# Two layers of feature-map attention and a gated unit: row sums for seven slabs by one TensorE operation, with a realignment through DRAM

## The chip, the cores and the metric

One core of one Trainium2 chip runs the whole program. The metric is the device time of one execution in microseconds (us). Three executions of the kernel before took 391.33, 390.58 and 389.74 us (median 390.58). The profiled execution took 390.76 us; its span, from the first to the last instruction, is 389.0 us.

## What is computed

The input x has 2048 rows of 512 columns in bf16. Attention (A) and a gated unit (B) alternate, twice each, with the same weights in both layers:

```python
x = A_x
x = x + A(layernorm(x)); x = x + B(layernorm(x))
x = x + A(layernorm(x)); x = x + B(layernorm(x))
# A, 32 heads of width 16:
q, k, v = split(x @ wqkv)
pq, pk = q @ w_phi[h], k @ w_phi[h]
phi(p) = concat(softmax(p), softmax(-p))            # 32 features per head
kv, z = phi(pk)^T @ v, sum over rows of phi(pk)
A(x) = ((phi(pq) @ kv) / (phi(pq) @ z + 1e-6)) @ wo
# B, inner width 1376:
B(x) = (relu(x @ W_gate) * (x @ W_up)) @ W_down
```

The sums kv and z run over all 2048 rows, so the query side of a layer can't be ended before the key side of all its rows is done.

## The kernel before

**Tiles and slabs.** The 2048 rows are 16 tiles of 128, grouped in five slabs of 2, 4, 4, 4 and 2 tiles (L15); slab 0 has 256 rows, slab 1 has 512, slab 4 has 256. I write (0,2) for slab 2 of the first layer. x stays in SBUF (`x_sb`).

**The start.** The loads are issued at L708 to L730. w_phi is folded into the key and query weights by `fold` (L777): each of four column blocks of the weight has to be transposed, either by TensorE with an eviction (L783, L784, from a natural copy in `hT`) or by a transposing DMA issued on SyncE's queue (L702); the list XW says which blocks the DMA takes (L181: blocks 0 and 1 of the key weight, all four of the query weight). The block-diagonal form `BD` of w_phi is made at L762, and the products of L789 are evicted to `Wkp` and `Wqp` at L791.

**The key side** (`into_a`, L1238). Layer norm (L813: statistics on VectorE at L798, scale and shift on ScalarE at L840 or VectorE at L843) writes `ytile`. It is transposed into `yA` or `yG` by DMA (L848) or by TensorE (L677 with L855, L872 with L878). `keys` (L883) makes key and value products of a tile, the two exponentials on ScalarE (L900), sums of 16 on VectorE (L906), reciprocals on VectorE (L909) or as Ln and Exp on ScalarE (L912, L913), copies values out of PSUM (L916), scales them on POOL or VectorE (L920), and gathers kv and z on TensorE (L932) and VectorE (L942).

**The query side** (`out_of_a`, L1244). `sums` (L964) prepares `ZD` and `kvbd`. `queries` (L991) makes the products and exponentials `expq` (L1001). `attend` (L1004) needs, for each row and head, the softmax sums of both signs and their products with z, and does this for a slab of n rows in two TensorE operations called here the sums (stationary `ZO`) and the denominators (`ZD`). Each has 32 matmuls of n/4 columns (L1016), in four column positions of the array. The quarter of the rows is put on the partitions, so that both results lie on the same partitions: the sums are copied by ScalarE (L1050), then VectorE multiplies (L1058, the second operand straight from PSUM) and adds (L1060), ScalarE takes Ln and Exp (L1061, L1062), and VectorE makes the factors `aT` (L1063).

The factors are spread over the features: for slabs 0 and 1 by TensorE (L1137) with multiplications on VectorE from PSUM (L1155) or from a ScalarE copy (L1151, L1152); for slabs 2, 3 and 4 by DMA, two to DRAM (L1073) and eight back into `abT` (L1077), and multiplications on VectorE or POOL (L1122). Then follow the numerators (L1089), their evictions to `oT`, the product with `wo` (L1104), the residual and the next layer norm.

**The gated unit** (`glu`, L1189). Gate and up products (L1204), ReLU on ScalarE (L1211), the product on VectorE (L1213), the last 96 inner columns apart (`rest`, L1161; its transposing DMA is at L1186), then the down product (L1224) and the residual (L1159).

**What sets the order.** Every operation is recorded with the regions that it reads and writes and a cost. `Program.schedule` picks, for all engines together, the operation that can start first by these costs; a list of turns (TURNS, L185) breaks ties and gives the priority. `plan` turns the dependences into waits. Each engine then runs its list in order. SyncE's list holds nearly all DMA issues, so an issue that waits holds back the issues behind it. ENG (L24) says which engine takes an operation that more than one can do. The dictionary's costs of DMAs are constants of `Program`; they change the order of the lists and no instruction. The two operations of the sums already have a second form in the code, at L1025 to L1039, for slabs named in ZALL; this list is empty (L184).

Of the kernel before, what the change touches and what calls it, by code (L numbers as in the profile page):

```python
# [12 lines left out]
P = 128  # L13
# [10 lines left out]
ENG = {'ap/a00/0': 'act',  # L24
 'ap/a01/3': 'dve',
 'ap/a02/2': 'dve',
# [3 lines left out]
 'ap/a10/0': 'act',  # L30
 'ap/a11/0': 'act',
 'ap/a11/3': 'act',
 'ap/a12/1': 'act',
 'ap/a12/2': 'act',
 'ap/a12/3': 'act',
 'ap/a13/1': 'act',
 'ap/g01/1': 'act',
# [3 lines left out]
 'ap/g03/1': 'act',  # L41
# [3 lines left out]
 'ap/g04/1': 'act',  # L45
 'ap/g11/1': 'act',
 'ap/g11/3': 'act',
 'ap/g12/3': 'act',
 'ap/g13/2': 'act',
 'ap/g13/3': 'act',  # L50
 'ap/g14/0': 'act',
 'ap/g14/1': 'act',
 'em/00/01': 'dve',
 'em/01/01': 'dve',
 'em/10/01': 'dve',
 'em/10/03': 'dve',
 'em/11/03': 'dve',
# [4 lines left out]
 'es/04/1': 'pool',  # L62
 'es/04/2': 'pool',
 'es/04/3': 'pool',
 'es/12/1': 'pool',
 'es/13/0': 'pool',
 'es/13/1': 'pool',
 'es/13/2': 'pool',
 'es/13/3': 'pool',
 'es/14/0': 'pool',  # L70
 'es/14/2': 'pool',
 'fcq0': 'dve',
 'fcq2': 'dve',
 'ld/wk2': 'sp',
 'ld/x1': 'act',
 'ot/00/3': 'act',
 'ot/01/1': 'dve',
 'ot/01/3': 'dve',
 'ot/02/1': 'dve',
 'ot/02/3': 'dve',  # L80
 'ot/03/1': 'dve',
 'ot/04/2': 'dve',
 'ot/10/0': 'dve',
 'ot/10/2': 'dve',
 'ot/10/3': 'act',
 'ot/11/1': 'dve',
 'ot/12/0': 'dve',
 'ot/12/2': 'dve',
 'ot/13/3': 'dve',
 'ot/14/2': 'dve',  # L90
 'rz/0/12': 'act',
 'rz/0/13': 'act',
 'rz/0/14': 'act',
 'rz/0/4': 'act',
 'rz/0/6': 'act',
 'rz/0/9': 'act',
 'rz/1/11': 'act',
 'rz/1/12': 'act',
 'rz/1/14': 'act',
 'rz/1/15': 'act',  # L100
 'rz/1/3': 'act',
 'rz/1/4': 'act',
 'rz/1/5': 'act',
 'rz/1/8': 'act',
 'vc/0/13': 'dve',
 'vc/0/3': 'dve',
 'vc/0/6': 'dve',
 'vc/0/7': 'dve',
 'vc/1/1': 'dve',
 'vc/1/11': 'dve',  # L110
 'vc/1/12': 'dve',
 'vc/1/2': 'dve',
 'vc/1/3': 'dve',
 'vc/1/5': 'dve',
 'vc/1/6': 'dve',
 'vc/1/8': 'dve',
 'vh/0/10/1': 'dve',
 'vh/0/12/1': 'dve',
 'vh/0/13/1': 'dve',
 'vh/0/14/0': 'dve',  # L120
 'vh/0/15/0': 'dve',
 'vh/0/15/1': 'dve',
 'vh/0/6/1': 'dve',
 'vh/0/8/0': 'dve',
 'vh/0/8/1': 'dve',
 'vh/1/0/0': 'dve',
 'vh/1/1/0': 'dve',
 'vh/1/10/0': 'dve',
 'vh/1/11/0': 'dve',
 'vh/1/12/0': 'dve',  # L130
 'vh/1/14/1': 'dve',
 'vh/1/15/0': 'dve',
 'vh/1/15/1': 'dve',
 'vh/1/2/0': 'dve',
 'vh/1/4/0': 'dve',
 'vh/1/4/1': 'dve',
 'vh/1/5/0': 'dve',
 'vh/1/5/1': 'dve',
 'vh/1/7/0': 'dve',
 'vh/1/8/0': 'dve',  # L140
 'vh/1/9/0': 'dve',
 'vh/1/9/1': 'dve',
# [4 lines left out]
 'yc/a00/1': 'dve',  # L147
 'yc/a01/00': 'act',
 'yc/a01/03': 'act',
# [22 lines left out]
 'yc/g11/03': 'act',  # L172
# [3 lines left out]
 'yc/g14/03': 'act'}  # L176
XPOSE = ('a02', 'a03', 'a04', 'a11', 'a12', 'a13', 'g01', 'g02', 'g03', 'g12', 'g13', 'g04', 'g14')
XISSUE = 1270.0
XDELAY = 215.0
BIG = 'sp'  # L180
XW = {'k': (0, 1), 'q': (0, 1, 2, 3)}  # L181
ZKPE = ()
FUSEZ = ()
ZALL = ()  # L184
TURNS = """  # L185
-28 300 427 180 240 186 0 614 40 120 554 928 1235 801 988 674 1362 1422 1115 1175 1482 1602 1662 1782 1542 1722 56 6 0 84 174 104 211 54 124 64 144 76
119 161 204 247 290 332 375 91 76 117 191 242 218 696 181 629 635 640 646 680 726 732 737 743 805 801 806 812 818 886 845 850 856 861 903 778 784 790
795 838 867 873 878 884 1009 241 357 386 424 542 570 663 668 674 680 728 299 373 405 440 252 318 560 566 571 771 980 1002 1023 1090 1306 1327 1366
1387 1141 1237 1318 1484 1477 1550 1656 959 1045 1067 1112 1219 1241 1263 1284 1189 1381 1598 1772 1429 1943 1837 1923 2201 2737 1794 1842 1848 1908
1955 1349 1355 1360 1539 1573 1653 1702 1854 1859 1895 1609 1615 1642 1647 1733 36 549 48 534 638 756 580 764 793 828 896 963 1002 934 1003 1072 970  # L190
1165 1333 1250 1284 1285 1729 1750 1799 1821 1772 2019 2062 2084 2092 1906 2287 2529 2237 2594 2700 1431 1452 1517 1659 1409 1544 1620 1680 1858 1800
2014 2187 1814 2252 2358 1474 1495 1566 1587 1865 1976 1997 2105 1685 1637 2629 2776 2808 2189 2953 2847 2329 2394 2416 2437 1707 1886 1954 2040 2535
2487 2794 2962 2140 3165 3059 2868 3304 3441 838 1243 1069 1526 1185 1533 1127 1706 1781 1848 1881 1888 1954 2023 2122 2155 2232 2462 2428 2495 2395
2643 2664 2772 2815 2600 2621 2686 2708 2870 2918 3004 3246 3310 2902 3349 3741 2729 2751 2949 2971 3100 3187 3208 3230 3069 3021 3177 3384 3324 3561
3455 3014 3036 3057 3079 3122 3144 3165 3273 3262 3129 3476 3692 3327 3906 3843 2794 2837 2928 2992 3364 3429 3450 3472 3444 3511 3584 3790 3993 3559
4137 4031 3892 4328 4505 2229 2779 1426 1874 1714 2787 1540 2772 2825 2860 3112 3317 3177 3375 3804 3285 3270 3524 3856 3397 3537 3559 3580 3602 3623
3645 3688 3710 3732 3684 3969 4095 3876 4243 4349 3839 3952 3973 4016 4038 4060 4081 4103 4066 4114 4187 4355 4162 4455 4561 4124 4146 4168 4189 4211
4232 4431 4517 4287 4239 4397 4602 4667 4619 4705 4818 3775 3818 3861 3995 3667 3731 3753 3796 4410 4506 4579 4734 4799 4295 4944 4881 4700 5235 5352
3119 3426 3492 3626 3734 3807 3983 2571 3433 3607 3780 3836 3924 4110 4254 4276 4297 4388 4582 4604 4647 4668 4554 4458 4687 4819 4884 4751 5163 5050
4409 4452 4539 4770 4474 4496 4560 4625 4836 4900 4973 5099 4686 5226 5289 5285 5412 5465 5515 5559 5525 2589 4759 4868 4998 5117 5150 5182 5215 5363  # L200
5315 3493 3504 3515 3526 4857 4901 4912 4987 5027 5075 5474 5531 5605 5662 5697 5751 5783 5821 5875 5998 6092 5939 5949 6058 6384 6456 6476 6486 6516
6550 6572 6593 6748 6812 6926 7073 6615 6636 6726 6769 6791 6868 6977 7011 7044 7121 7208 7272 7278 7284 7289 7326 6984 7025 7063 7095 7185 7191 7196
7202 7273 2127 2148 2170 2308 2358 2406 2567 3252 3385 3407 3636 4009 2459 2481 2502 2524 2632 2583 2286 2351 2373 2545 2680 2728 4801 4948 5630 5725
5773 5813 5850 5893 6232 6543 6304 6383 6340 6602 6090 6151 6147 6509 6244 6196 6443 6668 6749 6808 6797 6749 7295 7316 7338 7360 7419 6990 7033 7208
7251 7595 6925 7055 7076 7098 7148 6947 6968 7012 7229 7360 7537 7771 7713 7793 7655 7786 7479 7778 7822 7895 7941 7927 7934 8111 8093 7955 8024 8302
8429 8048 8175 7414 7597 7616 7625 7917 7947 8097 8138 8210 8278 8676 7381 7392 7477 7488 7532 7542 7586 7633 7786 7797 8117 8127 8147 8158 8168 8179
7672 8219 7422 7433 7444 7564 7575 7753 7764 7808 7403 7709 7840 7873 7895 7906 7925 7936 7847 7975 7499 7666 7687 7698 7731 7742 7829 7884 7955 7966
8010 8021 8032 8065 8223 8234 8348 8431 7510 7521 7553 7644 7655 7775 7851 8054 7676 7819 7862 8075 8086 8106 8201 8212 8300 8372 7455 7466 7605 7720
7977 7988 7999 8043 8190 8245 8256 8267 8278 8289 8343 8805 8162 8845 8321 8354 8375 8397 8551 8573 8594 8616 8927 8949 9357 9407 8300 8419 8440 8462
8646 8676 8697 8719 8971 8992 9039 9089 9587 9706 9175 9249 9735 9809 9893 9921 10033 10068 10255 13237 13259 13269 13340 14966 14988 15096 15290  # L210
13392 13441 13519 13682 15390 15624 15463 15074 15441 15873 15916 12933 13019 13062 13154 15966 16014 16107 16287 13198 16347 16410 19480 19501 19560
5052 5074 5096 5128 5219 5267 4944 5161 5381 5509 5559 5607 4879 4966 5009 5031 5123 5171 4923 5193 5338 5359 5411 5459 5733 5871 6002 6211 6363 6436
6594 6636 6751 6691 7087 7207 7327 7267 7027 6907 6967 7147 7827 7887 7389 7603 8493 8622 8633 8574 8574 9601 9688 9709 10076 10126 9753 9904 10012
10163 10259 8762 8784 8816 8838 8904 9731 9796 9817 9839 9900 10201 10319 10334 10408 8979 9053 9975 10099 10438 10473 10505 10558 10557 10621 10589
10991 10610 10864 10737 9298 9306 9487 9495 9504 9555 9563 9571 9608 9714 8638 8667 8903 8911 8919 9014 9022 9030 9067 9148 9881 9276 9422 9465 9925
10184 10271 10292 10379 9990 10429 9512 9623 9645 9666 9082 9444 9533 9580 9761 9833 8859 9190 9211 9233 9168 9255 9314 9401 9283 9467 9947 10098
10120 10228 10249 10314 10336 10400 10510 10654 10530 10552 10573 10595 9860 9882 9968 9990 10645 10717 8741 8881 9060 9103 10638 10660 10681 10703
9548 10776 10357 10444 10465 10487 10141 10422 10508 10616 10734 10836 9125 9147 9336 9379 11159 11246 11289 11375 10798 11425 9774 10033 10055 10206
10987 11051 11073 11138 10857 11188 10724 10746 10789 10832 10767 10811 10854 10875 10917 11047 12184 12205 12227 12249 12270 12317 12363 12385 12436
12458 12479 12609 13472 13523 13552 13667 14036 14134 14255 14367 14380 14402 14509 14619 10965 11008 11030 11116 11267 11311 11332 11656 11699 11894  # L220
# [132 lines left out]
class Program:  # L353
    SYNC = 120.0
    SAME = 60.0
    DMA_ISSUE = {"sp": 600.0, "act": 560.0, "pool": 1100.0}
    DMA_LAT = 1800.0
# [971 lines left out]
```

## Time and profile before

| | us |
|---|---|
| median of three runs | 390.58 (389.74 to 391.33) |
| profiled execution | 390.76 |
| its span | 389.0 |
| TensorE matmul busy | 373.5 (96% of the span) |
| VectorE busy | 275.5 |
| ScalarE busy | 193.8 |
| GpSimd (POOL) busy | 66.6 |
| DMA moved | 24.33 MB in 53067 packets |
| granted TensorE clock | 1.00 |

How to read it: busy times of matmuls overlap, since one matmul starts to stream before the one before it has left the array. A TensorE that is 96% busy can therefore still be slower than it could be; the distance between the starts of matmuls in a row tells how fast they really go. Over the span, the first 77 us are the key side and the first slabs of the first layer, about 190 to 262 us hold the key side of the second layer and its first slabs, and the gated unit fills most of the rest.

### The profile page before, as it was taken

What the parts mean: (1) busy time and instruction counts of PE and PEld (TensorE: products, weight loads), DVE (VectorE), ACT (ScalarE), POOL (GpSimd) and SP (SyncE); (2) the same over time, 40 slices, a digit from 0 to 9 for tenths busy, and PEclk for the clock granted to TensorE, in tenths of its full rate; (3) what the DMA queues carried; (4) which work ended last, traced back from release to release, by engine and by line L of the source; (5) the groups of instructions that cost most, each with busy time, mean ns of one, the idle gap of its engine ahead of it and who ended that gap; (6) DMA issues with size and microseconds to landing.
All of it is one profiled execution on the core that took longest, in us unless ns stands there. A gap on an engine that the chain in (4) does not pass through costs nothing.

```text
span 389.0 us, 9735 instructions
## 1 busy us (share of the span) xinstructions
PE 373.5 (96%) x4097; PEld 201.7 (52%) x4151; DVE 275.5 (71%) x561; ACT 193.8 (50%) x432; POOL 66.6 (17%) x59
## 2 busy tenths in 40 slices
PE   6999998999999999999999999999999999999996
PEld 3555455584444444454456555558444454444574
DVE  8999988885973676994359997899778234344343
ACT  4899899562360334393135659975153213212320
POOL 0168440151310000121003124003530000000000
PEclk9999999999999999999999999999999999999999
DMA  9992200224340000431000200015540201010111
GB/s 211 297 357 46 48 3 3 90 72 112 109 68 2 13 0 15 95 56 40 0 3 17 48 16 17 4 60 133 133 108 15 45 11 41 27 29 28 42 34 54
DMA packets 53067, 24.33 MB, mean 63 GB/s; under 512 B 38976, under 2 KB 52000, under 8 KB 53024
## 3 DMA queue, kind: packets, MB, share of 16 engines
q1 hardware_dynamic: 52208, 23.51, 24.2%
q8 instruction: 32, 0.52, 0.6%
q10 hardware_dynamic: 816, 0.21, 0.3%
q14 instruction: 11, 0.09, 0.1%
HBM read 12.89 MB, written 2.42 MB: 39 GB/s over the span
## 4 chain that ended last, share of the span: by engine, by line
PE 85%; ACT 4%; DMA 3%; DVE 3%; issue 2%; SPq 1%
PE pb L673 80%; DMA yG<-ytile 2%; ACT expk L900 2%; PE pb L932 2%; PE pb L1016 1%; DMA x_sb<-in_A_x_dram 1%; DVE expq L1155 1%; PE pb L1089 1%; SPq L848 1%; ACT expq L1001 1%; DVE stats L798 0%; ACT gate_sb L1211 0%; ACT ytile L840 0%; DVE oT L771 0%; PE pb L872 0%
## 5 line engine op out<-in xcount | busy, mean ns | idle before, releaser
L673 PE MATMUL pb<-yG,Wg 128*128 128x512 bf16 (+1 forms) x394 | 100.3, 336 | 1.1 <-DMA yG<-ytile 0.7
L673 PE MATMUL pb<-yG,Wu 128*128 128x512 bf16 (+1 forms) x393 | 98.6, 336 | 0.6 <-issue 0.3
L1211 ACT ACTIVATE gate_sb<-pb 128x512 bf16<-128x512 f32 x80 | 47.1, 596 | 104.3 <-PE pb L673 81.5
L673 PE MATMUL pb<-Wd,hT 128*128 128x512 bf16 (+2 forms) x352 | 97.1, 373 | 1.5 <-issue 0.9
L1213 DVE TENSOR_TENSOR hT<-gate_sb,pb 128x512 bf16<-128x512 bf16 x80 | 53.7, 683 | 53.9 <-PE pb L673 39.2
L920 POOL TENSOR_TENSOR vhat<-vsb,rZk 128x544 bf16<-128x544 bf16 x38 | 41.1, 1101 | 140.9 <-DVE x_sb L1159 48.1
L1159 DVE TENSOR_TENSOR x_sb<-x_sb,pb 128x512 bf16<-128x512 bf16 x59 | 39.4, 679 | 29.3 <-PE pb L673 28.9
L673 PEld LDWEIGHTS pb<-yG,Wg 128*128 128x128 bf16 x400 | 39.0, 98 | 31.2 <-issue 1.0
L673 PEld LDWEIGHTS pb<-yG,Wu 128*128 128x128 bf16 x400 | 38.9, 98 | 30.4 <-DVE hT L1213 0.2
L673 PEld LDWEIGHTS pb<-Wd,hT 128*128 128x128 bf16 (+1 forms) x363 | 35.0, 98 | 35.6 <-issue 2.0
L900 ACT ACTIVATE expk<-pb 128x512 bf16<-128x512 f32 x64 | 35.5, 603 | 21.7 <-PE pb L673 18.2
L906 DVE TENSOR_REDUCE Zk<-expk 128x64 f32<-128x1024 bf16 x32 | 38.4, 1204 | 3.8 <-ACT expk L900 3.8
L798 DVE BATCH_NORM_STATS2 stats<-x_sb 128x6 f32<-128x512 bf16 x60 | 39.8, 682 | 0.6 <-DMA x_sb<-in_A_x_dram 0.3
L1122 POOL TENSOR_TENSOR expq<-expq,abT 128x1024 bf16<-128x1024 bf16 (+1 forms) x14 | 24.8, 1777 | 79.8 <-DMA abT<-spread 24.5
L673 PE MATMUL pb<-Wkp,yA 128*128 128x512 bf16 x124 | 37.3, 390 | 0.8 <-issue 0.5
L673 PE MATMUL pb<-wv,yA 128*128 128x512 bf16 x122 | 35.0, 379 | 0.4 <-issue 0.2
L673 PE MATMUL pb<-wo_sb,oT 128*128 128x512 bf16 x121 | 34.7, 379 | 0.6 <-DVE stats L798 0.2
L1001 ACT ACTIVATE expq<-pb 128x512 bf16<-128x512 f32 x64 | 34.9, 628 | 0.6 <-PE pb L673 0.4
L673 PE MATMUL pb<-yA,Wqp 128*128 128x512 bf16 (+1 forms) x147 | 32.0, 333 | 2.0 <-issue 1.0
L840 ACT ACTIVATE ytile<-x_sb,nmr,rstd 128x512 bf16<-128x512 bf16 x33 | 25.7, 814 | 3.2 <-DVE nmr L832 3.2
L673 PE MATMUL pb<-Wl,yG 128*128 128x192 bf16 x128 | 21.6, 246 | 0.7 <-DMA yG<-ytile 0.6
L673 PEld LDWEIGHTS pb<-yA,Wqp 128*128 128x128 bf16 x160 | 14.3, 98 | 11.4 <-issue 0.2
(87 smaller groups left out, 323.8 us busy)
## 6 DMA issues: line engine op xcount, KB each, us to landing
abT<-spread SPq DMA_DIRECT2D x32, 128.0 KB
out_dram<-x_sb SPq DMA_DIRECT2D x15, 128.0 KB, 1.7
x_sb<-in_A_x_dram SPq DMA_DIRECT2D x3, 512.0 KB
Wg<-in_B_W_gate_dram SPq DMA_DIRECT2D x1, 1280.0 KB, 7.4
Wu<-in_B_W_up_dram SPq DMA_DIRECT2D x1, 1280.0 KB, 10.1
Wd<-in_B_W_down_dram SPq DMA_DIRECT2D x1, 1280.0 KB, 12.7
abT<-spread SPq DMA_DIRECT2D x16, 64.0 KB
wv<-in_A_wqkv_dram SPq DMA_DIRECT2D x1, 512.0 KB
```

What stands on the lines that cost most here:

```text
L673: op("pe", lambda e: e.matmul(view(ps), lhsT, rhs, start=start, stop=stop), reads=reads, writes=[ps], occ=max(25.0, 0.4167 * n + 2.6), lat ...
L798: op("dve", lambda e: e.bn_stats(stats[:, t, :], src()), reads=[res], writes=[R("st", t)], occ=580, lat=680, name=f"bn{t}")
L840: op("act", (lambda t, yb: lambda e: e.activation(ytile[:, yb, :], x_sb[:, t, :], ACT.Identity, bias=nmr[:, t, :], scale=rstd[:, t, :]))(t ...
L900: op("act", (lambda i, s, pk: lambda e: e.activation(expk[:, i, s, :], full(pk), ACT.Exp, scale=1.0 - 2.0 * s))(i, s, pk), reads=[pk], wri ...
L906: op("dve", (lambda i, zb: lambda e: e.tensor_reduce(Zk[:, zb, :], expk[:, i, :, :].rearrange("p s (h f) -> p (s h) f", f=16), AX.X, ALU.a ...
L920: op(eng, (lambda i, s, vb, rz: lambda e: e.tensor_tensor(vhat[:, i, s, :, :], vsb[:, vb, :, :], rZk[:, rz, s * 32:(s + 1) * 32].unsqueeze ...
L932: ins = e.matmul(ps.f32()[32 * i:32 * i + 32, g * 34:g * 34 + 34], expk[:, tiles[j], sg, f0:f0 + 32], vhat[:, tiles[j], sg, 8 * c + 2 * i: ...
L1001: op("act", (lambda c0, s, ps: lambda e: e.activation(eqv(st)[:, c0:c0 + per, s, :], ps.f32()[:, 0:per * n].rearrange("p (c n) -> p c n", ...
L1122: op(eng, lambda e: e.tensor_tensor(part, part, abT[:, c].rearrange("p (s n) -> p s n", s=2)[:, :, 0:n], ALU.mult), reads=Re + [R("abT", c ...
L1159: op("dve", lambda e: e.tensor_tensor(x_sb[:, t, :], x_sb[:, t, :], full(ps), ALU.add), reads=[R("x", t), ps], writes=[R("x", t)], occ=597 ...
L1211: op("act", (lambda gb, pg, k: lambda e: e.activation(gate_sb[:, gb, 0:k], pg.f32()[:, 0:k], ACT.Relu))(gb, pg, k), reads=[pg], writes=[R( ...
L1213: op("dve", (lambda gb, hb, pu, k: lambda e: e.tensor_tensor(hT[:, hb, 0:k], gate_sb[:, gb, 0:k], pu.f32()[:, 0:k], ALU.mult))(gb, hb, pu, k),
```

## The change

1. **One operation for the sums.** ZALL names seven slabs: (0,2), (0,3), (0,4), (1,1), (1,2), (1,3), (1,4). For these, the 64 matmuls of n/4 columns become eight of n columns: stationary `ZA` has, for each sign and group of eight heads, 32 columns, eight heads with four kinds of result (sum of this sign, sum of the other sign, two denominators). All four kinds then lie on different partitions, so the result is evicted from PSUM as 128 x n in FP32 into `abT` (ScalarE, or VectorE for (0,3), (1,2), (1,4)), written to a DRAM scratch by one DMA, and read back by a second DMA so that the kinds lie on the same partitions again. The two DMAs stand in SyncE's list; the multiplication then reads both operands from SBUF. There is one scratch, and `abT` is also what the spreading DMAs of slabs 2 to 4 write. Making `ZA` adds a memset, two copies and, per layer, two small multiplications on VectorE.
2. **The key weight.** XW takes all four blocks of the key weight by transposing DMA; two natural loads, eight TensorE transposes and two evictions go. All four evictions of `Wkp` are on ScalarE now (two were on VectorE).
3. **The first loads.** SyncE's list begins with x tile 0, w_phi, two key blocks, wv, x tiles 8 to 11, two key blocks; x tiles 2 and 3, 4 to 7, and 1 are issued by ScalarE, in this order. Before, SyncE issued x tile 0, tiles 2 and 3, 4 to 7, the two natural blocks and the two transposed ones, and ScalarE issued tile 1 and w_phi.
4. **Small work on POOL.** Four memsets and `BD` go from VectorE to POOL.
5. **Order and engines.** The DMA costs of `Program` are other numbers, and TURNS and ENG are other lists; so the order on every engine differs throughout, and some evictions, reciprocals and scalings are on other engines. In the second layer, slab (1,1) ends its query side behind the first matmuls of the gated unit of slab (1,0), where before it was ahead of them.
6. A switch TRUNC, off, that would leave out the later stages.

The core of the diff (TURNS and most of ENG left out; line numbers of the changed file are about 30 higher):

```diff
-XISSUE = 1270.0
-XDELAY = 215.0
+XISSUE = 1310.0
+XDELAY = 140.0
-XW = {'k': (0, 1), 'q': (0, 1, 2, 3)}
+XW = {'k': (0, 1, 2, 3), 'q': (0, 1, 2, 3)}
-ZALL = ()
+ZALL = ((0, 2), (0, 3), (0, 4), (1, 1), (1, 2), (1, 3), (1, 4))
+LATE = 300.0
...
-    DMA_ISSUE = {"sp": 600.0, "act": 560.0, "pool": 1100.0}
-    DMA_LAT = 1800.0
-    DMA_BW = 270.0
+    DMA_ISSUE = {"sp": 630.0, "act": 500.0, "pool": 1100.0}
+    DMA_LAT = 2000.0
+    DMA_BW = 360.0
...
-                begin = max(s + 0.35 * self.DMA_LAT, qfree)
+                begin = max(s + 0.75 * self.DMA_LAT, qfree)
-                o.finish = qfree + 0.65 * self.DMA_LAT + o.lat
+                o.finish = qfree + 0.25 * self.DMA_LAT + o.lat
...
+ 'ld/wphi': 'sp',
+ 'ld/x2': 'act',
+ 'ld/x4': 'act',
+ 'ms/BD': 'pool',
+ 'ms/ZD 0': 'pool',
+ 'ms/kvs 0 1': 'pool',
+ 'ms/kvs eps 1': 'pool',
+ 'ms/vsb ones': 'pool',
+ 'fck1': 'act',
+ 'fck3': 'act',
+ 'za/03': 'dve',
+ 'za/12': 'dve',
+ 'za/14': 'dve'
```

The code that the seven slabs now take, which both files have (the delays are costs of the planner alone):

```python
def all_sums(e):
    for s in range(2):
        for c in range(NC):
            ins = e.matmul(zd.f32()[32 * c:32 * c + 32, 0:n], ZA[:, s, c, :], eqv(st)[:, c, s, :],
                           start=s == 0, stop=s == 1, tile_position=(0, 32 * c))
    return ins
...
evict(ENG.get(f"za/{L}{st}", "act"), lambda: Zn, lambda: zd.f32()[:, 0:n], n, zd, [], R_Zn, f"zac{st}")
dma("sp", lambda e: e.dma_start(zscr[:, 0:n], Zn), reads=R_Zn, writes=[R("zscr")], nbytes=512 * n, name=f"zao{st}", delay=LATE)
zk = Zs[:].rearrange("p g n -> p (g n)")[:, 0:4 * w].rearrange("p (k w) -> p k w", w=w)
dma("sp", lambda e: e.dma_start(zk, zscr[:, 0:n].rearrange("(h k) (q w) -> q h k w", k=4, w=w)), reads=[R("zscr")], writes=[R("Zs", 0), R("Zs", 1)], nbytes=512 * n, name=f"zai{st}", delay=LATE)
```

## Prediction

> **What bounds the kernel.** I read the busy times by stage first, because the page's single line for TensorE (96% busy) hides where it is slow. Columns: stretch in us and its length, then busy time and count of TensorE matmuls, weight loads, VectorE, ScalarE and POOL, the granted clock, the DMA share and GB/s.
>
> ```profile
> 0.00:12.00 12.00, 8.44 (x43) 4.59 (x44) 10.29 (x37) 7.12 (x15) 0.78 (x7) 1.00 0.98 234
> 12.00:50.00 38.00, 36.56 (x604) 18.45 (x609) 37.11 (x71) 34.41 (x78) 21.52 (x20) 1.00 0.61 172
> ...
> 57.00:77.00 20.00, 18.50 (x514) 10.49 (x519) 16.55 (x43) 16.42 (x44) 0.49 (x1) 1.00 0.12 39
> 77.00:92.00 15.00, 14.20 (x140) 10.49 (x140) 10.40 (x26) 7.12 (x15) 5.84 (x3) 1.00 0.38 75
> 92.00:190.00 98.00, 97.36 (x534) 46.27 (x543) 69.93 (x139) 38.86 (x81) 11.04 (x9) 1.00 0.22 48
> ...
> 228.00:246.00 18.00, 17.36 (x389) 9.77 (x392) 14.25 (x28) 17.14 (x44) 4.32 (x4) 1.00 0.09 18
> 246.00:262.00 16.00, 15.31 (x383) 9.05 (x386) 14.77 (x36) 13.39 (x36) 0.00 (x0) 1.00 0.11 32
> ```
>
> From 92 to 190 us, the gated unit, TensorE is the bound and others idle: only less TensorE work helps. From 12 to 50 us VectorE is busy 37.11 of 38 us: it is the bound, ScalarE (34.41) close behind. From 57 to 77 nobody is full: there the chain of waits runs from ScalarE's exponentials through VectorE's multiplications to TensorE. From 228 to 246 ScalarE is the bound (17.14 of 18). So the same saving is worth different things by stage. Second, TensorE's order in time around the sums (start, length, instruction, count, idle before):
>
> ```profile
> 62.12 0.94 PE L673 MATMUL pb<-yA,Wqp 128*128 128x256 bf16 x7
> 62.99 0.63 PE L1016 MATMUL pb<-expq,ZD 128*32 128x128 bf16 x32
> 63.55 0.39 PE L673 MATMUL pb<-yA,Wqp 128*128 128x256 bf16 x2
> ...
> 66.67 0.44 PE L1089 MATMUL pb<-expq,kvbd 32*32 32x256 bf16 x32 [0.15 <-DVE expq L1155]
> 67.04 0.42 PE L1016 MATMUL pb<-expq,ZO 128*32 128x64 bf16 x32
> 67.69 0.81 PE L673 MATMUL pb<-yA,Wqp 128*128 128x512 bf16 x3 [0.24 <-DVE expq L1155]
> ...
> 69.51 0.65 PE L1089 MATMUL pb<-expq,kvbd 32*32 32x512 bf16 x32
> 70.10 0.82 PE L673 MATMUL pb<-wo_sb,oT 128*128 128x512 bf16 x3
> ```
>
> From start to next start, a set of 32 matmuls of 128 columns takes 0.56 us (62.99 to 63.55). One of 64 columns takes 0.24 to 0.41; I use 0.30. The numerators take 0.59 (32 of 512 columns) and 0.37 (32 of 256). Plain 512-column matmuls come every 0.215 us (in the chain, 49 in 10.74 us with one record missing).
>
> **One operation for the sums.** The trace has no set of eight 128-row matmuls of 512 columns in four column positions. If the four overlap, it is two rounds of 512 columns, 0.43 us; if nothing overlaps, 8 x 0.215 = 1.72. Nearest are the numerators, also two rounds of 512 columns: 0.59 (and 0.37 for 256). I take these, since today's 32 x 128 columns at 0.56 (17 ns each, where 128 columns alone stream in 54) already overlap in the same four positions. Five slabs save 2 x 0.56 - 0.59 = 0.53, two save 2 x 0.30 - 0.37 = 0.23, together 3.1. One return to full matmuls fewer per slab, each with 0.16 us idle in the timeline, adds 7 x 0.16 = 1.1. TensorE loses 4.2 us of work; without overlap it would gain 5 x 0.60 + 2 x 0.26 - 1.1 = 2.4.
>
> ScalarE's copy (0.406 and 0.315) becomes an eviction of twice the columns (0.63 by the `abT` row), three of seven on VectorE. The multiplication now reads SBUF only; by its row 0.418, and I leave it there.
>
> **The new wait.** The eviction goes to DRAM and back. Per slab: eviction 0.63, DMA out, DMA in, then 0.42 + 0.29 + 0.32 + 0.34 + 0.42 for the unchanged small steps and some 0.8 for hand-overs: 3.2 us and two landings. The landing is known from these rows:
>
> ```profile
> out_dram<-x_sb SPq DMA_DIRECT2D x15, 128.0 KB, 1.7
> ...
> DMA to landing us min/median/max: 2.4/2.5/4.4
> ```
>
> The second is that of the transposing DMAs of `ytile`. With 1.7 to 4.4 each, the detour takes 6.6 to 12.0 us; I take 2.5, since two passes of 256 KB are nearest to the transposes in packets: 8.2. Cover, from the changed order on TensorE: the tightest is (1,1), where between its sums and its spread stand 8 + 13 + 8 + 1 matmuls of 512 columns (6.5 us), 16 of 256 at 0.108 (1.7), 8 of `Wl` (0.7) and slab 0's numerators, its transposes and the sums of slabs 2 and 4 (about 1.8): 10.7 us. The others have more than 15. So I cost the detour at nothing; at the upper end it is 1.3 us late once. Behind the waiting multiplication stand, on VectorE, the gated unit's products and residuals; behind a waiting issue on SyncE, the transposes that the next gated unit needs.
>
> **Start.** Blocks 2 and 3 of the key weight now land by transposing DMA. Ahead of block 3's issue SyncE has 0.40 + 0.46 + 2.60 + 0.52 + 0.58 + 1.30 us of issues (x tile 0, w_phi, two blocks, wv, x tiles, block 2), so it begins at 0.8 + 5.9 + gaps 0.4 = 7.1, and lands 4.4 later (the row of the six weight transposes, 3.9 to 4.6): 11.5. Fold and eviction end at 12.6, where before the first key matmul started at 11.0. TensorE fills with wv matmuls, 8 x 0.215 = 1.7, that came later before. First exponential, 13.89 before: +0.5 us, between -1 and +1.5. The eight transposes saved were in a stretch where TensorE waited: nothing. DMA engines are 98% busy to 12 us (above). [...]
>
> **12 to 57 us.** Counting VectorE's list up to `kvbd` in both orders, by each row's mean: four reciprocals less (-2.17), two `Wkp` evictions (-1.38), `BD` (-0.68), transpose evictions (-1.64), memsets (-0.7), against four value copies (+2.72), a scaling (+0.76), `ZA` (+0.55) and small ones: 64.0 becomes 61.7. ScalarE gains 0.7 on 34.41 of 38. VectorE is the bound, so up to -2.3; with ScalarE that near I take -1.5, from -2.3 to 0.
>
> **57 to 92 us.** Three slabs change: TensorE -(2 x 0.53 + 0.23 + 3 x 0.16) = -1.8; VectorE's list up to the first `hl` product falls by another 3.5, as multiplications of later slabs move behind. I take TensorE's -1.8, from -3.5 to 0. The wait for `yG` at 87 to 90.7 (chain: SyncE 0.70, DMA 3.71) may shift by -1.5 to +4; taken at 0.
>
> **228 to 280 us.** Four slabs: -(3 x 0.53 + 0.23 + 4 x 0.16) = -2.5 on TensorE, and between the layers' gated units ScalarE's list goes from 93 to 87 instructions (41.6 to 40.3 us by rows), VectorE's from 85 to 60, as (1,1) ends later. I take -2.5, from -4 to 0. **Gated units:** 0, as VectorE (70 of 98) has room for what comes; up to +3.
>
> **Sum:** 0.5 - 1.5 - 1.8 - 2.5 = -5.3 from the profiled 390.76 (span 389.0 and 1.76 around it): 385.5. That execution is 0.18 above the median, so the same against 390.58 is 385.3; I keep 385.5.
>
> **Rivals.**
> 1. *Late realignment, slower.* If the multiplication waits for its DMA at the head of VectorE's list, gate products stop, and TensorE runs on for one free pair of banks, about 1.7 us (16 matmuls of 256 columns). At 4.4 us per landing each detour is 3.8 later than I take, 2.1 beyond that cover; in the four detours where DMA is otherwise busy (77 to 92, 262 to 280: shares 0.38, 0.51) that is +8.4: 385.5 + 8.4 = 393.9. It decides once total lateness passes 5.3 us, 0.76 per slab. For it: the `yG` wait already ends on SyncE's list at 87 us. Against: 10.7 us cover and more. Chance 0.18.
> 2. *The saving is hidden.* If the chain through ScalarE keeps its length in the 57 and 228 us stages, nothing stays of their 4.3: 389.8. For it: ScalarE 17.14 of 18. Chance 0.22.
> 3. *No overlap of the eight matmuls:* 4.2 + 2.4 = 6.6 more than forecast, 392.1. Against: 17 ns per matmul today. Chance 0.03.
> 4. *Start worse:* block 3 lands later and VectorE's backlog doesn't catch up, +1.5 in place of +0.5 and nothing of the -1.5: 388.0. Chance 0.07.
> Forecast: 0.50.
>
> A difference under 0.5% (2 us) can't be told from no change here. Faster: the forecast, case 4 mostly and a part of case 2: 0.60. Same: 0.20. Slower: 0.20. Range: 381.5 (rather more than half of the 7.0 that the lower ends would add) to 391.5, which leaves out most of case 1 and a low tail.
>
> **What would show it.** Right: 8-matmul sets at about 0.59; VectorE under 36.5 of 38 in 12 to 50; the first gate matmul of layer 2's slab 0 some 5 us earlier; no multiplication waiting for a DMA. Wrong: first exponential after 15.5 us; VectorE waiting at the multiplication for `Zs`; new waits of TensorE for `yG`; sums over 1 us.

## The result and the profile after

| | us | against before |
|---|---|---|
| before | 390.12 median (388.81 to 391.33, 12 runs) | |
| changed kernel | 393.63 median (391.25 to 398.36, 12 runs) | ratio 1.0094, 95% interval [1.0067, 1.012] |

The forecast was 385.5; the change made the kernel 0.94% slower. The profiled execution of the changed kernel, one of the two slow ones among the twelve, took 397.73 us (span 396.0), 4.1 above the median, so its trace shows the loss larger than the typical run has it.

Busy times by stage in the changed kernel, columns as before (the third number from the right is the granted clock):

```profile
0.00:12.00 12.00, 7.05 (x25) 2.88 (x26) 9.59 (x35) 6.05 (x13) 2.79 (x12) 1.00 0.94 224
12.00:50.00 38.00, 37.30 (x625) 19.58 (x623) 36.24 (x65) 36.26 (x87) 19.85 (x19) 1.00 0.71 175
57.00:77.00 20.00, 18.60 (x357) 9.54 (x355) 16.00 (x42) 16.54 (x41) 0.00 (x0) 1.00 0.13 42
77.00:92.00 15.00, 15.00 (x141) 10.50 (x139) 10.20 (x24) 6.46 (x13) 6.33 (x3) 1.00 0.57 125
92.00:100.00 8.00, 5.97 (x20) 2.20 (x19) 5.01 (x12) 0.62 (x2) 0.00 (x0) 0.79 0.43 70
...
280.00:300.00 20.00, 18.05 (x86) 8.45 (x85) 10.93 (x27) 6.15 (x15) 0.00 (x0) 0.91 0.36 83
```

From 12 to 50 us VectorE is at 36.24 of 38, as forecast. Two later stretches stand out: 92 to 100 us has 20 matmuls at a clock of 0.79, and 280 to 300 has 86 at 0.91. The kernel before had 47 and 130 matmuls there, at 1.00. TensorE's order in time at the two places, and then VectorE's (the bracket is the idle time ahead and what ended it):

```profile
90.29 2.75 PE L697 MATMUL pb<-wo_sb,oT 128*128 128x512 bf16 x12
95.07 0.39 PE L697 MATMUL pb<-yG,Wg 128*128 128x512 bf16 x1 [2.03 <-DMA yG<-ytile]
...
287.30 0.33 PE L697 MATMUL pb<-Wl,yG 128*128 128x192 bf16 x2
289.57 0.39 PE L697 MATMUL pb<-yG,Wg 128*128 128x512 bf16 x1 [1.95 <-DVE hl L1210]
```

```profile
92.62 0.43 DVE L1085 TENSOR_TENSOR zm<-Zs 128x256 f32<-128x256 f32 x1 [3.63 <-DMA Zs<-sums_scr]
...
287.96 0.43 DVE L1085 TENSOR_TENSOR zm<-Zs 128x256 f32<-128x256 f32 x1 [2.19 <-DMA Zs<-sums_scr]
...
289.19 0.32 DVE L1210 TENSOR_TENSOR hl<-gate_sb,pb 128x192 bf16<-128x192 bf16 x1
```

The multiplication of the realigned sums (`zm`) stands at the head of VectorE's list and waits for the DMA that brings them back. At 287 us the gated unit's product `hl` stands behind it, and TensorE waits for `hl`. At 92 us TensorE waits for the transposed layer norm `yG`, whose DMA is on SyncE's list right behind the read back. All seven multiplications waited, 13.4 us in total (who waited for the tile `Zs`, us and times):

```profile
  DVE zm L1085: 13.4, 7
```

The chain that ended last names the transfer (start, length):

```profile
64.17 5.53 DMA Zs<-sums_scr
...
90.03 5.00 DMA yG<-ytile
...
248.89 1.99 DMA sums_scr<-abT
...
250.90 5.62 DMA Zs<-sums_scr
...
282.26 5.68 DMA Zs<-sums_scr
```

The write to DRAM takes 1.99 us, and the read of the same 256 KB 5.53 to 5.68. The reason can be read in the DMA share (second number from the right, of 16 engines). Two stretches of the changed kernel in which the read back, and little else, moves:

```profile
66.50:69.50 3.00, 2.71 (x51) 1.05 (x49) 2.30 (x5) 3.00 (x9) 0.00 (x0) 1.00 0.25 72
...
252.50:256.00 3.50, 3.50 (x22) 1.31 (x21) 2.67 (x6) 3.10 (x10) 0.00 (x0) 1.00 0.25 74
```

A share of 0.25 over 3 us can be four of the 16 engines busy all the time, or all 16 busy for a quarter of it. The trace's single packets decide for the first: in these stretches four packets of 512 bytes are under way at once (median; from 252.5 to 255.4 us never fewer than three), each for 27 ns, and the transfer ends with four packets of 4 bytes, where the write before it ends with 16. The rate is 72 to 74 GB/s. The read's pattern is `"(h k) (q w) -> q h k w"`: its outermost index q has four values. That this index sets the number of engines is my reading of the two fours; the first two runs below test it.

### The profile page after: what moved, and what is told of

Its sections match the earlier page's. It is cut to its first block, busy times and chain, and to the rows that moved or that the text cites. A ratio compares the mean times of both kernels' runs of the same rounds, so it can differ in the third digit from the quotient of the medians.

```text
span 396.0 us, 9018 instructions
## 1 busy us (share of the span) xinstructions
PE 379.1 (96%) x3751; PEld 197.0 (50%) x3751; DVE 272.7 (69%) x560; ACT 198.2 (50%) x445; POOL 63.1 (16%) x60
## 4 chain that ended last, share of the span: by engine, by line
PE 78%; DMA 11%; SPq 4%; DVE 4%; ACT 3%; issue 1%
PE pb L697 73%; DMA Zs<-sums_scr 8%; PE pb L962 2%; ACT expq L1031 2%; SPq L726 2%; DMA hT<-in_A_wqkv_dram 1%; DMA yG<-ytile 1%; PE pb L1119 1%; DVE x_sb L1189 1%; SPq L878 1%; DVE hT L1243 1%; DMA sums_scr<-abT 1%; DVE zm L1085 0%; PE pb L1046 0%; SPq L720 0%
## 5 line engine op out<-in xcount | busy, mean ns | idle before, releaser
L697 PE MATMUL pb<-yG,Wg 128*128 128x512 bf16 (+1 forms) x400 | 97.4, 346 | 4.4 <-DMA yG<-ytile 2.0
L697 PE MATMUL pb<-yG,Wu 128*128 128x512 bf16 (+1 forms) x400 | 95.8, 337 | 0.0
L697 PE MATMUL pb<-Wd,hT 128*128 128x512 bf16 (+2 forms) x363 | 94.8, 373 | 0.3 <-DVE hT L1243 0.3
L1152 POOL TENSOR_TENSOR expq<-expq,abT 128x1024 bf16<-128x1024 bf16 (+1 forms) x11 | 20.3, 1861 | 146.3 <-PE pb L697 59.8
L697 PE MATMUL pb<-wv,yA 128*128 128x512 bf16 x128 | 40.0, 387 | 0.5 <-ACT rstd L857 0.5
L697 PE MATMUL pb<-Wkp,yA 128*128 128x512 bf16 x128 | 39.3, 381 | 0.1
L697 PE MATMUL pb<-yA,Wqp 128*128 128x512 bf16 (+1 forms) x160 | 34.6, 338 | 0.0
L697 PE MATMUL pb<-wo_sb,oT 128*128 128x512 bf16 x128 | 32.6, 379 | 0.2 <-ACT oT L804 0.2
L870 ACT ACTIVATE ytile<-x_sb,nmr,rstd 128x512 bf16<-128x512 bf16 x31 | 23.9, 812 | 6.0 <-DVE nmr L862 6.0
L1209 ACT ACTIVATE gate_sb<-pb 128x192 bf16<-128x192 f32 x16 | 5.2, 328 | 39.1 <-PE pb L697 39.1
```

The source lines that it names most:

```text
L697: op("pe", lambda e: e.matmul(view(ps), lhsT, rhs, start=start, stop=stop), reads=reads, writes=[ps], occ=max(25.0, 0.4167 * n + 2.6), lat ...
L870: op("act", (lambda t, yb: lambda e: e.activation(ytile[:, yb, :], x_sb[:, t, :], ACT.Identity, bias=nmr[:, t, :], scale=rstd[:, t, :]))(t ...
L1152: op(eng, lambda e: e.tensor_tensor(part, part, abT[:, c].rearrange("p (s n) -> p s n", s=2)[:, :, 0:n], ALU.mult), reads=Re + [R("abT", c ...
```

## Experiments

The edits are shortened to what counts. Each run stands against the kernel before on its own chip, whose median was 389.49 to 389.98 us there and 390.12 in the result above, so differences between runs of different chips are also given by these ratios.

### Realign on the way out

```diff
-dma_start(zscr[:, 0:n], Zn)
+dma_start(zscr[0:128*n].rearrange("(q p w) -> p q w", q=4, w=w),
+          Zn.rearrange("p (q w) -> p q w", q=4))
-dma_start(zk, zscr[:, 0:n].rearrange("(h k) (q w) -> q h k w", k=4, w=w))
+dma_start(Zs_flat[:, 0:4*w], zscr[0:128*n].rearrange("(p m) -> p m", m=4*w))
```

> The changed kernel with one edit: the realignment is done by the write to DRAM instead of by the read back. The write now scatters pieces of 512 bytes (256 bytes for slabs of 256 rows), partition by partition; the read back takes 128 whole rows of 2 KB. Everything computed, and every list of instructions, stays. Theory A (the read back is slow because its pattern begins with an index of only four values, and what it delays behind it): the read back lands in 2.2 to 3.0 us instead of 5.5 to 5.7, the write in at most 3.0, eviction to multiplication of slab 1 of the second layer about 8 us instead of 10.6, VectorE's waits for the sums under 5 us in all instead of 13.4, no idle time of TensorE above 1 us at 92 or at 287 us, no granted clock below 1 before the end, and 389.3 us (388.3 to 390.3). Theory B (the transfers are late because SyncE's list and the rings are crowded there, whatever the pattern): the read back still takes over 4.5 us and the time stays at 392.5 to 394. Theory C (something else in the new order costs the time, at the start or in the gated units): landings get short but the time stays above 391.5.

Measured: **386.69 us** (386.42 to 387.14), ratio to before 0.9936 [0.9921, 0.9952]. The view of the read back's line in this run (who waited for it, us and times; issue to landing):

```profile
  DVE zm L1085: 2.2, 2
...
DMA to landing us min/median/max: 2.1/2.5/3.2
```

The read back lands in 2.1 to 3.2 us. Its share of the engines while it moves, and below it the write's, for slab (0,2):

```profile
64.99:66.28 1.29, 0.97 (x22) 0.64 (x21) 1.29 (x4) 1.29 (x4) 0.00 (x0) 1.00 0.67 203
62.53:63.57 1.04, 1.04 (x7) 0.39 (x4) 1.04 (x3) 1.04 (x3) 0.00 (x0) 1.00 0.89 252
```

That is 11 and 14 engines on average where the slow read kept four. VectorE waits 2.2 us in two multiplications instead of 13.4 in seven, and TensorE has no idle time over 1 us after the first 9 us. Both stretches of idle time are whole again:

```profile
92.00:100.00 8.00, 8.00 (x48) 4.25 (x46) 6.94 (x17) 1.44 (x4) 0.23 (x1) 1.00 0.34 115
...
280.00:300.00 20.00, 20.00 (x99) 9.39 (x98) 9.66 (x23) 7.95 (x17) 4.20 (x2) 1.00 0.35 95
```

Theory A holds and B falls: the list and the queues are the same, and the transfer is short. My number for it was 2.6 us too high: I had taken off the two stalls of TensorE alone, and not the other waits, and 0.6 of it is the chip, on which the kernel before took 389.49. This is a version faster than both kernels.

### The same read, in four

```diff
-dma_start(zk, zscr[:, 0:n].rearrange("(h k) (q w) -> q h k w", k=4, w=w))
+for q in range(4):
+    dma_start(zk[32*q:32*q+32], zscr[:, q*w:(q+1)*w].rearrange("(h k) w -> h k w", k=4))
```

> The changed kernel with the read back issued as four DMAs, one for each quarter, each of 32 partitions by 4 pieces; the write and the pieces of 512 bytes stay as they were. Everything computed stays. Each read back costs three issues more on SyncE's list, 0.57 us each. Theory A (the order of the pattern's indices makes it slow, not the size of its pieces): the four land within 3.5 us of the first issue's end, the two idle times of TensorE go, and the time is 390 us (389 to 391.5), a little above the edit that reads whole rows. Theory B (crowded list and rings): 393 to 395, since the list grows longer.

Measured: 390.19 us (389.71 to 390.89), ratio 1.0021 [1.0008, 1.0035]. Each quarter lands 2.1 to 3.1 us after its issue (median 2.3). The pieces are the same 512 bytes, so their size was not the matter; the outermost index is now 32. But the four issues, 0.60 us each, follow one another: in the four read backs that are on this run's chain, the last quarter lands 3.9 to 5.0 us after the first issue began. VectorE still waits 9.1 us in four multiplications, with 1.29 us of idle TensorE at 282.6, which the expectation had as gone. It is 3.5 us behind the realigning write: about half of the loss is regained. That the issues keep the rest is the likely reading; the later landing and the longer list of SyncE were not taken apart.

### Nobody waits; nothing moves

```diff
-Zsv, Zdv = zk[:, 0:2], zk[:, 2:4]
+Zsv = Zdv = fixed[:, 0:w].unsqueeze(1).to_broadcast([P, 2, w])   # ones
```

> The changed kernel, but the two VectorE products after the sums (denominators, and the scaling by the reciprocal) take a constant tile of ones instead of the sums read back; both DMAs of the detour still run, in the same places, and only the next slab's detour waits for them. This leaves out the sums and denominators of the seven slabs. Theory A: VectorE's waits for the read back are gone (13.4 us before), so the idle time of TensorE at 287 us goes; the transfers queued behind the 5.6 us read back are still late, so some of the idle time at 92 us stays (over 0.5 us); 390 us (389 to 391.5). Theory C (the wait is not what costs): above 392.5.

Measured: 387.25 us median, ratio 0.9951 [0.9934, 0.9969]. With the four-engine read still running, 0.91 us of idle time stays at 92 us, again for `yG`, as expected; the time is 2.8 us lower than I had put it, much as with the realigning write. In the next run the two DMAs move one row of 2 KB each:

```diff
-dma_start(zscr[:, 0:n], Zn)
+dma_start(zscr[0:1, 0:n], Zn[0:1])
-dma_start(zk, zscr[:, 0:n].rearrange("(h k) (q w) -> q h k w", k=4, w=w))
+dma_start(zk[0:1], zscr[0:1, 0:n].rearrange("p (k w) -> p k w", k=4))
```

> As the run without the wait, and in addition the two DMAs of each detour move a single row of 2 KB instead of 256 KB, so that nothing queues behind them; the issues stay. This leaves out the sums and denominators of the seven slabs. It is the floor of what any faster detour can reach with this order. Theory A: both idle times of TensorE gone, clock 1 up to the end, 388.5 us (387 to 389.5), within 1 us of the edit that reads whole rows. If it is over 2 us below that edit, what is left of the detour still costs that much. Theory C: above 391.

Measured: 386.22 us (385.84 to 386.9), ratio 0.9927 [0.9904, 0.995]. That is 2.3 us under the 388.5 that I had put. So, of the 393.63 - 386.22 = 7.4 us that the detour costs the changed kernel (6.5 by the ratios), the waiting is 6.4 (to 387.25; 5.6 by the ratios). About 1.0 is left for what the slow read does to other transfers, and 0.5 is what the realigning write leaves (386.69 - 386.22). These last two are no larger than the noise, since the intervals of the three runs overlap. A detour through DRAM of the right shape is nearly free here.

### The rest of the change, without the one operation

Turns of the old operations stand where the new ones had theirs:

```diff
-ZALL = ((0, 2), (0, 3), (0, 4), (1, 1), (1, 2), (1, 3), (1, 4))
+ZALL = ()
```

> The changed kernel without its first part: sums and denominators of all slabs by the old two operations and no detour through DRAM, with the new start and the new engine choices kept; turns of the seven slabs' old operations are those of the new ones, so the order of the rest is that of the changed kernel but for small shifts. It separates the start and the new order from the sums. Theory: the seven single operations are worth about the 2.7 us of TensorE work by which the two traces differ and some of its changes of mode, 3 to 4 us, so this run is that much above the run whose read back takes whole rows (386.7): 390 us (389 to 391.5), near the kernel before, and no idle time over 1.5 us in the middle. Rival: the gain of that run comes from the start and the engine choices; then this run is also below 388.

Measured: 390.93 us (389.93 to 392.89), ratio 1.0034 [1.0017, 1.005]. The seven single operations are thus worth 390.93 - 386.69 = 4.2 us when their detour is short (by the two ratios to before, 1.0034 - 0.9936 = 0.98%, 3.8 us), and the start and the new order together cost 390.93 - 389.71 = 1.2. The order was made for the single operations, though, so a part of either number can come from old operations standing in places that were not planned for them. The rival falls: without the sums nothing is gained.

### The start

In the kernel with the realigning write, two key weight blocks go back to plain loads and TensorE transposes:

```diff
-XW = {'k': (0, 1, 2, 3), 'q': (0, 1, 2, 3)}
+XW = {'k': (0, 1), 'q': (0, 1, 2, 3)}
```

> The run with the realigning write, but key weight blocks 2 and 3 are loaded plainly and turned by TensorE and two evictions, as in the kernel before; SyncE's list keeps its places, with two plain issues of about 0.5 us for two of 1.3. Theory (turning by DMA costs at the start, where the first exponential came at 16.17 us against 13.89, and the key side, on which VectorE is full, gives back what it gave): the first exponential at 14.5 to 15.7 us, and the time 0 to 1.5 us below the run it is made from. Rival (the turned weight is what makes up for the late start, by two evictions and eight transposes less): 0.5 to 2 us above it.

Measured: 389.23 us (387.21 to 391.96), ratio 0.9986 [0.9963, 1.0008]. Beside it:

> The run with the realigning write once more, beside the run with the plain key loads on the same chip: 386.7 us (386 to 387.4).

Measured: 386.28 us (385.66 to 386.62), ratio 0.9911 [0.9884, 0.9938]. So undoing this part costs 2.9 us, and my theory of it falls. The first exponential came at 16.87, not earlier than the 16.17 and 16.47 of the two runs with the turned weight. (In its profiled execution the granted clock is 0.50 from 8.46 to 15.29 us; in that of the changed kernel, with the turned weight too, the clock records begin at 13.83 us with full clock. So a part of this may be the clock.) In this order of the rest, the turned key weight helps. What in the new start and order then costs the 1.2 us of the run without the sums, this doesn't say: the order of loads and the engine choices were not taken apart, and this stays open.

### An idle time put in by hand

Both stretches of the changed kernel lose more than the idle time. The granted clock, by stretches of 3.413 us laid on its own steps (changed kernel: ahead of each fall, and in it):

```profile
92.33:95.75 3.41, 1.39 (x8) 0.43 (x6) 2.97 (x7) 0.62 (x2) 0.00 (x0) 1.00 0.59 38
95.75:99.16 3.41, 3.41 (x10) 1.21 (x9) 2.04 (x6) 0.00 (x0) 0.00 (x0) 0.50 0.26 77
...
286.89:290.31 3.41, 1.47 (x10) 0.74 (x9) 2.11 (x8) 1.06 (x4) 0.00 (x0) 1.00 0.18 56
290.31:293.72 3.41, 3.41 (x10) 1.22 (x8) 1.86 (x7) 2.08 (x6) 0.00 (x0) 0.50 0.28 58
```

To test it, one matmul of the kernel before is made to wait:

```diff
+dma("sp", lambda e: e.dma_start(idle[:], x_sb[:, 0, 0:256]), writes=[R("idle")])
+late.deps = {run[k].idx}         # issued when matmul k is done
+run[k + 1].deps.add(late.idx)    # matmul k+1 waits for it
```

> The kernel before with one stall put in by hand: in the dense stretch of gated units near 135 us one matmul waits for a small DMA that is issued only when the matmul ahead of it is done (64 KB from SBUF to SBUF into a tile of its own); every list of instructions stays in order. TensorE should sit idle for 2.0 to 2.6 us. Theory A (an idle time of about 2 us costs more than itself, since the granted clock falls to 0.5 for 3.4 us after it): the clock row shows 0.5 for 3.4 us in at least some of the runs, and the time is 3.5 to 4.3 us above before in those. Rival (the falls seen in the changed kernel come of something else): clock 1, and 2.0 to 2.6 us above before.

Measured: 392.56 us (391.39 to 395.0), ratio 1.0075 [1.0049, 1.0102]: 2.85 us for 1.97 us of idle time at 139.6, with the clock at 1.00 around it in the profile. Neither number was hit; the interval covers 1.9 to 4.0 us.

> As the long stall, but the matmul waits for four small memsets on GpSimd instead, at the same place: 0.7 to 1.4 us of idle time. Theory A: no fall of the clock, since idle times up to 1.3 us in the other traces had none, and the time rises by no more than the idle time itself, 0.5 to 1.4 us. Rival: any idle time in a dense stretch sets the clock back, and it rises by 1.7 us more.

Measured: 389.91 us, ratio 1.0003 [0.9989, 1.0016]. The idle time came out at 0.53 us, shorter than meant, and the clock stayed at 1; it costs nothing that can be measured. It excludes only that any gap sets the clock back.

> The kernel before with the stall by hand made twice as long: two small DMAs, one after the other, between the same two matmuls near 135 us. In the traces so far the granted clock is cut in stretches of 3.413 us on a fixed grid, and falls to 0.5 for one stretch when TensorE was busy for less than about 1.5 us of the stretch before (1.39 and 1.47 in the changed kernel, 0.68 and 0.66 at the start of others: falls; 1.53, 1.65, 1.96, 2.02: none); the single stall of 1.96 us lay across an edge of that grid, 0.5 and 1.45 us on its sides, and had none. Theory: an idle time of 4 us leaves less than 1.5 us of work in one stretch wherever the grid lies, so the profile shows 0.5 for 3.4 us (or twice that) right after, and the time is before + 4 + 1.7, 5 to 6.5 us above. Rival: no fall, 3.5 to 4.5 us above.

Measured: 395.73 us (394.97 to 396.75), ratio 1.0149 [1.0115, 1.0182]: 5.75 us (the interval covers 4.5 to 7.1) for 3.87 us of idle time, which with half of 3.413 makes 5.58. Its windows:

```profile
139.64:143.05 3.41, 0.00 (x0) 0.00 (x0) 1.04 (x2) 0.60 (x1) 0.00 (x0) 1.00 0.13 38
143.05:146.47 3.42, 3.41 (x9) 1.21 (x10) 1.56 (x3) 0.00 (x0) 0.00 (x0) 0.50 0.00 0
146.47:150.00 3.53, 3.53 (x18) 1.65 (x17) 1.82 (x4) 1.04 (x2) 0.00 (x0) 1.00 0.00 0
```

Nine matmuls at 0.50 where eighteen fit: the fall follows the idle time, and not the change. In the changed kernel, gaps of 2.03 and 1.95 us were enough, where one stretch of 3.413 us had under 1.5 us of work (1.39 and 1.47).

This is not what makes the changed kernel slower, though: three of its runs with a mean clock of 1.0 took 392.65, 393.56 and 393.7. The two falls, 1.7 us each, could be most of the 4.1 by which the profiled execution lies above the median; but four other runs with the same mean clock, 0.991, took 391.25 to 394.06, and where their clock fell isn't on record.

## Why the prediction was wrong, step by step

**The new wait (wrong; the main cause of the miss).** The step said "I take 2.5, since two passes of 256 KB are nearest to the transposes in packets: 8.2", and costed the detour at nothing. The write came at 2.0 to 2.6. The read back came at 5.5 to 5.7 for slabs of 512 rows, because it ran on four of the 16 DMA engines (share 0.25), which I hadn't looked for in its pattern. In (1,1) the eviction begins at 248.21 and the data lies at 256.52, 8.3 us later; with the realigning write it is 5.8 (243.16 to 248.9), and by the step's own terms 0.63 + 2.5 + 2.5 = 5.6. (The 8.2 of the step is the whole detour, with the small steps behind the landing.) A second fault is in the cover: I counted TensorE's work between the sums and the spread, but what counts is where the multiplication stands in VectorE's list. (0,3), with "more than 15" us by my count, waited longest, 3.63. At 2.5 us per landing this fault hardly shows (2.2 us of waits, no stall); at 5.6 it decides.

**Rival 1 was the outcome.** It named the mechanism, the multiplication at the head of VectorE's list with gated products behind it, and 393.9 us; 393.63 was measured. That the number is so near is partly luck: it set four detours, 2.1 us late each, on a base of 385.5, where seven waits cost 6 to 7 us on a base of about 386.7. It had a chance of 0.18, worked out with two landings of 4.4; the true pair is 2.5 and 5.6, almost the same sum. Its upper landing was a real row of the trace, and I should have asked which of the two transfers had a reason to be slow.

**One operation for the sums (right).** The changed kernel's sets:

```profile
60.47 0.60 PE L1059 MATMUL pb<-expq,ZA 128*32 128x512 bf16 x8
...
67.59 0.62 PE L1059 MATMUL pb<-expq,ZA 128*32 128x512 bf16 x8
```

They last 0.60 and 0.62; from start to next start, as the 0.59 was read, it is 0.54 (60.47 to 61.01). For the two stages the forecast had 1.8 + 2.5 = 4.3 us less; the runs with and without the single operation differ by 3.8 to 4.2.

**Start (wrong in size).** First exponential +2.33 us (13.89 to 16.22), outside -1 to +1.5: the transposing loads that I put at 4.4 us show 6.5 where the trace has a landing. The step also took matmuls of 512 columns at 0.215 us each. In the changed kernel, two of them:

```profile
11.82 0.63 PE L697 MATMUL pb<-wv,yA 128*128 128x512 bf16 x1
...
16.27 0.38 PE L697 MATMUL pb<-wv,yA 128*128 128x512 bf16 x1
```

The early ones start 0.43 apart (11.39 to 11.82), the later ones 0.22 (14.10 to 14.32). The trace's clock records begin only at 13.83 us (13.39 in the kernel before), so the 1.00 that the views print ahead of that was not measured; by these matmuls TensorE ran at half its rate there, in both kernels (before: starts 0.43 apart up to 13.12 us, 0.22 from 13.47 on).

**12 to 57 us:** VectorE came to 36.24 of 38, under the 36.5 named, but the last gathering matmuls of the key side end at 57.78 against 57.60 before (57.66 with the realigning write), where the two terms said 1.0 earlier. Gain and late start cancel; the forecast had counted 1.1 to 1.2 us too many.

**57 to 92 us (right, once the wait is gone).** First `Wl` matmul of the first layer: 76.99 before, 76.32 after, 75.32 with the realigning write. Counted from the end of the key side, that last is 1.7 less than before; 1.8 was forecast. **The `yG` wait, "taken at 0":** +2.03 us of idle time and a clock fall behind it in the profiled execution, so near the upper end of its -1.5 to +4; with the short read it is gone.

**228 to 280 us (right as far as can be told) and gated units (wrong).** The first gate matmul of the second layer came 3.8 us earlier (262.2 to 258.4), against "some 5 us"; with the short read 9.8 (252.4). In both, the end of slab (1,1)'s query side now stands behind this matmul, where before it stood ahead, so not all of it is time gained. Of the 4.3 us by which the profiled execution with the short read is shorter (389.0 to 384.7), 1.7 are there at 75 us and 2.6 come later, where 2.5 was forecast. "Gated units: 0" failed in the changed kernel by the stall at 287 us.

**Sum.** With the read back at the length assumed, the kernel takes 386.69 and 386.28. That is 2.8 and 3.7 us below the kernel before on the same chips, of 5.3 forecast. By the profiled executions some 1.1 us of what is missing lies in the start and the key side; where the rest, 0.5 to 1.4, lies is open. The term that turned the forecast gain into a loss is the landing of the read back, put at 2.5 and measured at 5.5 to 5.7, with the wait behind it put at nothing: 393.63 - 386.69 = 6.9 us, or 6.2 by the ratios.

## What to carry to other kernels

Before a DMA is costed by a row of another, read its pattern from the outermost index: with four values there, this one ran on four of the 16 engines (share 0.25), and turning the realignment into the write, whose pattern begins with 128 partitions, made it 2.5 us instead of 5.6 for the same bytes. Measure the cover of a new wait where the waiting instruction stands in its engine's list, not where its result is needed. And look at the DMA share while a long transfer moves alone: the flat 0.25 here meant that 12 of the 16 engines had no part in it.

## What the runs showed of the hardware that I had not expected

- In the traces of the two kernels the granted clock changes only on a fixed grid of 3.413 us: in the changed kernel at 95.75, 99.16, 290.31 and 293.72 us, the last three 1, 57 and 58 steps behind the first. It fell to 0.5 for the next step or two where TensorE was busy for 0 us of one (the double stall, g3_double), 0.66 (e4_nodata), 0.68 (a0_nosums), 1.39 and 1.47 (changed kernel); it didn't with 1.96 (behind the single stall, g1_long). So the bound lies between 1.47 and 1.96 in these traces. I don't count the 1.53, 1.65 and 2.02 in the expectation of the double stall: they lie in the first 11 us, and in the traces of the two kernels the clock records begin only at 13.39 and 13.83 us. A stall of 1.97 us that lay across an edge (0.5 and 1.45 us on its sides) kept the clock, while 1.95 and 2.03 inside one lost it. The busy times are those of the profile, whose matmul ends are modelled.
- Four DMAs with 32 rows outermost moved together what one with four moved in 5.6 us, each landing in 2.3 (median); with the issues one behind the other, all were there 3.9 to 5.0 us after the first began. The price is three issues more at 0.60 us.
